# Reordering the first batch of a fused attention and mixer kernel: v by halves, s on a second queue, causal masks ahead of scores, masks of batch 1 on GpSimd

## The chip, the cores and the metric

The kernel runs on one core of a Trainium2 chip. The metric is the device time of one execution in microseconds (us), as a median over executions. Executions in which the time is over 1.5% above the fastest of the same kernel are called slow. A kernel is called faster or slower when it differs by 2%.

Five engines work side by side in this kernel, each on its own instructions in a fixed order: TensorE (PE, busy 278.1 of 293.2 us in the kernel before) multiplies matrices, ScalarE (ACT, 182.6) does exponentials and other functions, VectorE (DVE, 172.4) and GpSimd (POOL, 93.1) work elementwise, and SyncE (SP) issues most transfers. An engine whose next instruction waits is seen to do nothing else in the meantime, even if later instructions are ready: in experiment 1 below, ScalarE stands 12.04 us before one square, the last 3.70 of them with the scores of its next exponentials written (in the changed kernel it stands 12.10).

## The reference, cut to what matters

For 8 batches of 8 heads, 576 positions and 64 channels: attention with a decay, then a token mixer and a channel mixer.

```
cum    = cumsum(max(s, 0))
scores = q @ k.T / 8 + min(-(cum_i - cum_j), 0);  masked where j > i
x      = softmax(scores) @ v                       # heads side by side: 576 x 512
u      = x + (relu(x.T @ w_tok1) @ w_tok2).T
out    = u + relu(u @ w_ch1) @ w_ch2
```

## The kernel before

The decay is folded into the weights wn = exp(cum - half), which multiply v. A planner in the program models the duration of every operation and transfer, simulates the engines and fixes the order of instructions on each engine; the chip then runs that order. It makes six simulations ("passes") and keeps the one with the shortest modelled length.

Four heads form a quad. Its scores go into PSUM, ScalarE makes the exponentials, GpSimd or TensorE masks, and TensorE multiplies by v ("AV"). In batches below PMASK the mask is a matmul of the identity with a matrix of large negative numbers, added behind the scores:

```python
PMASK = 2
...
if pem:                                   # b < PMASK
    for e in range(HQ):
        for (jc, a, z, c0) in cols:
            n = min(128, S - jc * 128)
            nc.tensor.matmul(out=ps[e].t[:, c0 : c0 + n], lhsT=ident[:, :], rhs=neg[:, 0:n],
                             start=False, stop=(jc == cols[-1][0]))
```

To guard the arithmetic, ScalarE squares every loaded block of q and k and keeps the sums; a flag is made of them.

```python
def square(f, b, h, i):
    col = 2 * ((b * H + h) // HQ) + i
    P.op({"ACT": (1.1, 1.5, lambda: nc.scalar.activation(
        out=junk[:, :], in_=f.t[:, :], func=AF.Square, accum_out=sq[:, col : col + 1]))},
        reads=[(f, 0)], writes=[("sq", col)], prio=60)
```

## Time and profile before

| | before |
|---|---|
| time, median of 3 runs | 294.67 us (294.63 to 294.95) |
| span of the profiled run | 293.2 us |
| TensorE busy / idle | 278.1 / 15.1 us |
| granted TensorE clock | 1.00 in every window but the last |

TensorE is the bound. The columns are engine, line, releaser, then us in all, how often, and the longest:

```profile
ACT junk L645 <- DMA qkf<-in_k_dram: 5.7, 5, 1.9
ACT junk L645 <- DMA qkf<-in_q_dram: 4.6, 2, 4.4
```

ScalarE stands 10.3 us in front of squares whose q or k has not landed. TensorE's waits for exponentials come to only 0.4 us in this kernel, so the lines look harmless.

### The profile page before, as it was taken

To read this page: it belongs to the slowest core of one execution; us is meant where nothing else is said; L and a number is where in the kernel's file an instruction comes from. 1 tells how busy PE (TensorE), PEld (TensorE's weight loads), DVE (VectorE), ACT (ScalarE), POOL (GpSimd) and SP (SyncE) were. 2 spreads that over 40 slices of the span, in tenths; PEclk is the share of its full clock that TensorE was granted. 3 is DMA by queue.
4 is the path that set the end of the run, shared out by engine and by line. 5 is a ranking of instruction groups with operands and counts; after the bars stand their busy time and mean duration, and the time that the engine had idled before them with its cause. 6 is when DMAs were issued, how large, how long until landed. Compare 5 with 4: busy or idle time off the path is not lost.

```text
span 293.2 us, 6606 instructions
## 1 busy us (share of the span) xinstructions
PE 278.1 (95%) x2565; PEld 155.6 (53%) x2597; DVE 172.4 (59%) x332; ACT 182.6 (62%) x344; POOL 93.1 (32%) x138
## 2 busy tenths in 40 slices
PE   8779999989899979999999999999999999999994
PEld 3565466547554534446754545456754545347643
DVE  4974774989977635696847748596425523530022
ACT  3855875699896847975985278866872255007600
POOL 4332200878919312730481114821211210000000
PEclk9999999999999999999999999999999999999999
DMA  7998999999389999958493755667003320150023
GB/s 227 277 331 324 402 293 303 224 366 279 105 232 295 242 225 365 230 149 286 116 211 72 223 200 194 224 137 168 2 0 73 108 74 0 56 143 37 3 72 112
DMA packets 68051, 54.09 MB, mean 184 GB/s; under 512 B 53681, under 2 KB 56561, under 8 KB 68017
## 3 DMA queue, kind: packets, MB, share of 16 engines
q1 hardware_dynamic: 68016, 53.64, 64.6%
q8 instruction: 21, 0.34, 0.5%
q14 instruction: 14, 0.11, 0.1%
HBM read 40.65 MB, written 9.44 MB: 171 GB/s over the span
## 4 chain that ended last, share of the span: by engine, by line
PE 72%; DMA 9%; SPq 8%; DVE 6%; issue 2%; ACT 1%; POOL 1%; ACTq 0%
PE pmx L1078 26%; PE pmx L1052 25%; SPq L613 7%; PE pmx L994 4%; PE pmx L969 4%; PE pmx L744 4%; DMA ga<-in_moe_w_ch_dram 4%; PE psc L703 4%; DMA qkf<-in_k_dram 2%; DMA vf<-in_v_dram 2%; PE pmx L929 1%; DMA uTa<-ua 1%; PE psc L744 1%; DVE x L758 1%; DVE kT L670 1%
## 5 line engine op out<-in xcount | busy, mean ns | idle before, releaser
L719 ACT ACTIVATE E<-psc 128x512 bf16<-128x512 f32 x120 | 62.9, 602 | 20.9 <-PE psc L703 13.1
L1052 PEld LDWEIGHTS <-wc 128*128 128x128 bf16 x528 | 50.4, 98 | 35.0 <-issue 4.8
L727 POOL TENSOR_SCALAR_AFFINE_SELECT E<-E 128x512 bf16<-128x512 bf16 (+1 forms) x60 | 34.7, 608 | 87.0 <-ACT E L719 70.2
L1052 PE MATMUL pmx<-uTb,wc 128*128 128x320 bf16 x384 | 54.4, 299 | 1.1 <-DVE x L758 1.1
L1078 PE MATMUL pmx<-wc,gb 128*128 128x512 bf16 (+1 forms) x245 | 53.2, 369 | 0.5 <-issue 0.2
L1058 ACT ACTIVATE gb<-pmx 128x320 bf16<-128x320 f32 x79 | 34.3, 439 | 25.0 <-PE pmx L1052 18.1
L645 ACT ACTIVATE junk<-qkf 128x1152 bf16<-128x1152 f32 x32 | 37.3, 1165 | 10.7 <-DMA qkf<-in_k_dram 5.7
L1078 PEld LDWEIGHTS <-gb 128*128 128x128 bf16 x252 | 23.7, 98 | 25.4 <-issue 0.7
L620 POOL TENSOR_TENSOR vp<-vf,wT 128x512 bf16<-128x512 f32 (+1 forms) x30 | 32.1, 1100 | 9.2 <-PE pmx L744 9.2
L1052 PE MATMUL pmx<-uTa,wc 128*128 128x512 bf16 x137 | 32.4, 379 | 2.2 <-DMA uTa<-ua 1.8
L1078 PE MATMUL pmx<-wc,ga 128*128 128x512 bf16 x138 | 32.6, 379 | 0.4 <-issue 0.2
L659 POOL CAST qkb<-qkf 128x1152 bf16<-128x1152 f32 (+1 forms) x15 | 15.4, 1024 | 37.7 <-DMA qkf<-in_k_dram 16.4
L758 DVE TENSOR_TENSOR x<-pmx,rc 128x320 bf16<-128x320 f32 x52 | 25.5, 490 | 1.7
L744 PEld LDWEIGHTS <-E 128*128 128x128 bf16 x576 | 20.9, 97 | 6.8 <-DVE vp L620 1.7
L1058 ACT ACTIVATE ga<-pmx 128x512 bf16<-128x512 f32 x24 | 14.4, 599 | 15.6 <-PE pmx L1052 15.5
L670 DVE STREAM_TRANSPOSE kT<-qkb 128x576 f32<-128x576 f32 x16 | 20.1, 1255 | 5.7 <-PE psc L703 4.0
L1086 DVE TENSOR_TENSOR of<-pmx,ub 128x512 f32<-128x512 f32 (+1 forms) x17 | 11.2, 658 | 18.2 <-PE pmx L1078 14.4
L703 PE MATMUL psc<-qT,kT 32*128 32x256 bf16 (+2 forms) x592 | 20.1, 251 | 1.8 <-DVE qT L670 1.2
L1078 PEld LDWEIGHTS <-ga 128*128 128x128 bf16 x144 | 13.3, 98 | 15.6 <-issue 1.1
L670 DVE STREAM_TRANSPOSE qT<-qkb 128x576 f32<-128x576 f32 x16 | 20.0, 1247 | 1.6 <-ACT qkb L663 1.0
L703 PEld LDWEIGHTS <-kT 32*128 32x128 bf16 x640 | 13.6, 92 | 12.0 <-issue 10.2
L744 PE MATMUL pmx<-vp,E 128*128 128x65 bf16 x468 | 18.2, 193 | 0.0
(107 smaller groups left out, 285.1 us busy)
## 6 DMA issues: line engine op xcount, KB each, us to landing
qkf<-in_k_dram SPq DMA_DIRECT2D x20, 576.0 KB, 5.9
qkf<-in_q_dram SPq DMA_DIRECT2D x20, 576.0 KB, 6.1
vf<-in_v_dram SPq DMA_DIRECT2D x32, 256.0 KB, 5.8
out_dram<-of SPq DMA_DIRECT2D x31, 256.0 KB, 2.6
ga<-in_moe_w_ch_dram SPq DMA_DIRECT2D x6, 768.0 KB, 8.2
vf<-in_moe_w_ch_dram SPq DMA_DIRECT2D x2, 768.0 KB, 9.8
out_dram<-of SPq DMA_DIRECT2D x10, 128.0 KB, 2.7
vf<-in_v_dram SPq DMA_DIRECT2D x8, 128.0 KB, 4.9
```

The lines of the kernel that those rows point to most:

```text
L613: nc.sync.dma_start(out=vf.t[0:n, c, :, :], in_=v[b, :, c * 128 : c * 128 + n, :].rearrange("h p d -> p h d"))
L620: eng.tensor_tensor(out=vp.t[0:n, c, :, 0:D], in0=vf.t[0:n, c, :, :], in1=wT[0:n, c, b * H : b * H + H].unsqueeze(2).to_broadcast([n, H, D ...
L645: P.op({"ACT": (1.1, 1.5, lambda: nc.scalar.activation(out=junk[:, :], in_=f.t[:, :], func=AF.Square, accum_out=sq[:, col : col + 1]))}, r ...
L670: nc.vector.transpose(out=T.t[:, 0:S, :].rearrange("p s q -> p (s q)").bitcast(FP32).rearrange("p (t r) -> p r t", r=R), in_=t1.t[:, :].bi ...
L703: nc.tensor.matmul(out=ps[e].t[:, c0 : c0 + z - a], lhsT=kT.t[p0 : p0 + TP, jc * 128 : jc * 128 + 128, qq], rhs=qT.t[p0 : p0 + TP, a:z, qq ...
L719: nc.scalar.activation(out=E.t[:, e, ph * 512 : ph * 512 + 512], in_=p.t[:, :], func=AF.Exp, scale=0.125)
L727: nc.gpsimd.affine_select(out=w, in_=w, compare_op=ALU.is_ge, fill=0.0, base=0, pattern=[[0, HQ], [1, n]], channel_multiplier=-1)
L744: nc.tensor.matmul(out=o[:, ic, 0 : D + 1], lhsT=E.t[:, hh, d0 : d0 + 128], rhs=vp.t[:, jc, h + hh, 0 : D + 1], start=(jc == j_lo), stop=( ...
L758: nc.vector.tensor_tensor(out=x.t[:, :, (h + hh) * D : (h + hh + 1) * D], in0=o[:, :, 0:D], in1=rc.t[:, :].unsqueeze(2).to_broadcast([128, ...
L1052: nc.tensor.matmul(out=pm.t[:, 0 : e - a], lhsT=wc1[:, m, cc * 128 : cc * 128 + 128], rhs=uT.t[:, m, a:e], start=(m == 0), stop=(m == NMC ...
L1058: lambda cc=cc, pm=pm, a=a, e=e: nc.scalar.activation(out=g.t[:, cc, a:e], in_=pm.t[:, 0 : e - a], func=AF.Relu),
L1078: nc.tensor.matmul(out=pm.t[:, na:nb], lhsT=g.t[:, cc, c * 128 : c * 128 + 128], rhs=wc2[:, cc, na:nb], start=(cc == 0), stop=(cc == NCC - 1))
```

## The change

The intent is to start attention earlier and to relieve TensorE: s is loaded first, on ScalarE's queue; wn is made before the first exponentials; batch 0's masks are put into PSUM before the scores, while TensorE is waiting anyway; v of batch 0 is loaded by halves of the heads with w_tok1 between; masks of batch 1 go to GpSimd. The core of the diff:

```diff
-        etime = {"PE": 0.0, "ACT": 2.1, "DVE": 2.5, "POOL": 4.0, "SP": 0.7}
+        etime = {"PE": 0.0, "ACT": 2.86, "DVE": 2.5, "POOL": 4.0, "SP": 0.7}
-    PMASK = 2
+    PMASK = 1
-    stage_s = lambda: load_op(
-        lambda: nc.sync.dma_start(out=s_sb[:, :], in_=s...), ["s"], 1.0)
+    stage_s = lambda: early(
+        lambda: nc.scalar.dma_start(out=s_sb[:, :], in_=s...), ["s"], 3.5)   # 3.5: assumed landing
...                                              # relu of s from ScalarE to VectorE
+            def mask(ps=ps, cols=cols):          # ahead of the scores, 256 columns wide
+                for e in range(HQ):
+                    for (jc, a, z, c0) in cols:
+                        nc.tensor.matmul(out=ps[e].t[:, c0 : c0 + z - a], lhsT=ident[:, :],
+                                         rhs=neg[:, 0 : z - a], start=(c0 == 0), stop=False)
...
-    stage_qk(0, 0)
     stage_s()
     decay()
+    stage_qk(0, 0)
     stage_qk(0, HQ)
-    stage_v(0)
-    for h in range(0, H, HQ):
-        quad(0, h)
+    stage_v(0, 0)
+    quad(0, 0)
+    load_tok1(Buf(r_uTb))
+    stage_v(0, 1)
+    quad(0, HQ)
```

Because the planner starts anew, the order of instructions changes in all eight batches, not only in the first.

## The prediction

> **What bounds the kernel now.** I read the page first: TensorE (PE) is busy 278.1 of 293.2 us. So a gain has only two sources: matmul work that goes away, or some of the 15.1 us in which TensorE has nothing. I then cut the span into windows to find those 15 us.

> ```profile
> PE 278.1 (95%) x2565; PEld 155.6 (53%) x2597; DVE 172.4 (59%) x332; ACT 182.6 (62%) x344; POOL 93.1 (32%) x138
> ...
> 70.00:80.00 10.00, 8.80 (x111) 6.42 (x109) 9.79 (x22) 8.54 (x18) 9.95 (x11) 1.00 0.56 155
> ...
> 100.00:120.00 20.00, 18.06 (x146) 8.71 (x148) 10.15 (x20) 13.50 (x25) 4.54 (x7) 1.00 1.01 269
> ```

> Columns of a window: from:to, length, busy us of PE, PEld, DVE, ACT, POOL, then clock, DMA share, GB/s. Between 70 and 80 us VectorE (9.79) and GpSimd (9.95) are full and TensorE idles 1.2; between 100 and 120 it idles 1.9. From 20 to 50 us it idles only 0.25, from 120 to 280 only 1.5. The rest is the end (3 us after the last matmul) and the start.

> The start, from the timeline (start, duration, engine, line, operation, in brackets the idle time before and what ended it):

> ```profile
> 10.74 2.02 ACT L719 ACTIVATE E<-psc 128x512 bf16<-128x512 f32 x4
> ...
> 17.78 0.69 DVE L620 TENSOR_TENSOR vp<-vf,wT 64x512 bf16<-64x512 f32 x1 [1.34 <-DMA vf<-in_v_dram]
> 18.52 0.90 PEld L744 LDWEIGHTS <-E 128*128 128x128 bf16 x28 [1.65 <-DVE vp L620]
> ...
> 19.21 1.50 POOL L787 CAST w<-uTb 128x512 bf16<-128x512 f32 x3 [4.22 <-DMA uTb<-in_moe_w_tok_dram]
> ```

> Two chains meet at 18.5 us. ScalarE makes the sixteen exponentials back to back from 10.74 to 18.54 (0.485 each), and the last piece of v lands at 17.76, so E times v starts only at 18.52. A third follows: w_tok1 lands at 19.2, its casts end at 20.7, and the token mixing waits for them (first L864 at 20.78). Channel mixing (L906) runs steadily from 27.57. Much of TensorE's earlier busy time is warm-up on zeros (L1191, 25 records, 7.6 us).

> Then I asked what lies between 27 and 60 us, where TensorE never waits long:

> ```profile
> 31.36 12.37 SPq L613 DMA_DIRECT2D vf<-in_v_dram  x5
> 43.83 0.57 SPq L837 DMA_DIRECT2D ga<-in_moe_w_ch_dram  x1
> ...
> 50.68 0.96 DVE L789 CAST wc<-ga 128x1536 bf16<-128x1536 f32 x1 [2.86 <-DMA ga<-in_moe_w_ch_dram]
> ...
> 51.69 0.81 PE L929 MATMUL pmx<-wc,gb 128*128 128x512 bf16 x3 [0.27 <-DVE wc L789]
> ```

> The last quarter of w_ch2 is issued behind batch 1's v (12.37 us of issuing), lands at 50.66 and is cast by 51.64. TensorE needs it at 51.4 and waits 0.27. This is a second bound right behind the first: the transfers.

> ```profile
> 75.68 1.60 PE L1052 MATMUL pmx<-uTb,wc 128*128 128x320 bf16 x10 [1.06 <-DVE x L758]
> ...
> 96.56 6.43 SPq L1016 DMA_TRANSPOSE uTa<-ua  x4
> ...
> 104.58 1.02 PE L1052 MATMUL pmx<-uTa,wc 128*128 128x512 bf16 x4 [1.79 <-DMA uTa<-ua]
> ```

> The two single waits that I can see later. VectorE's chain up to the first holds the check's scan, gap and flag work (70.07 to 75) ahead of two normalisations; the second waits for transposes by DMA that were queued behind v loads.

> [...] v comes in 256-byte rows; in the trace the queue moves 222 GB/s from 10.4 to 14.7 us (v) and 400 from 27 to 40 us (mostly weights, k and q)[...]. [...] s on ScalarE's queue therefore frees 0.58 us of SyncE and moves s ahead[...]. [...] GpSimd's 128x576 cast takes 0.67 us, but 1.22 beside the scan, and its 128x32 copy 0.33, but 0.85 beside VectorE's v products. [...]

> **The change, part by part.** I compared the instruction order of both kernels on each engine, since a scheduler decides it.

> (1) s, cumulative sum and weights first. s landed at 7.73 and wn occupied ScalarE from 10.06 to 10.84, just ahead of the first exponential. With s ahead, relu (now VectorE), scan and wn lie near 4 to 7 us, beside the k and q loads. q's transpose still ends near 8.7 because q lands at 6.5, scores take 0.4 to 0.6 us, and the first exponential may start near 9.6 instead of 10.7: -1.1 for quad 0.

> (2) Masks of batch 0 ahead of scores. The mask groups (8 or 12 matmuls, 0.62 and 0.74 us each in the trace) leave the path between scores and exponentials. They get wider (up to 256 columns), but lie in warm-up time: -0.6, inside the 1.1 above. But the second quad's q lands at 10.7 as before, and its halves are now cast by GpSimd alone (2 x 0.67, after k's two and the copies of 0.33 and 0.21): transposed near 14.3, scores near 15. Eight exponentials from there (3.9) end near 19. So ScalarE gains no more than it lost, but AV of quad 0 can run at 16 to 17 instead of 18.5.

> (3) v by halves, w_tok1 between. Cumulated bytes: k and q done at 9.6 us, v's 1.18 MB took until 14.7 (0.23 MB/us), w_tok1's 0.59 MB some 1.6 us. Half a v is then through at 12.2 (landing, with the observed lag of 1 to 3 us, by 15), w_tok1 at 13.8 (landing near 16.3 instead of 19.2), the other half at 16.3 (landing near 19.1). AV of quad 1 can start at about 19.5, and one of four token chunks is done before. Left from there: AV 1.1 (36 at 0.03), three L864 groups (10 each at 0.088: 2.6), L877 4 x 0.23, L883 4 x 0.43: 6.4 us. Channel mixing starts near 26.0 instead of 27.57: **-1.5 us** at that point.

> (4) Masks of batch 1 by GpSimd. 40 matmuls of batch 1 go. Groups of 8 and 12 stand for 0.45 and 0.6 us of occupancy, twice each: **-2.2 us** of TensorE. Ten GpSimd selects (0.66 for 128x512) come in: 6 us, but GpSimd is idle from 38 to 52 us (0.67 busy in the slice 35 to 40, 0 in 40 to 50), so they cost latency only.

> (5) What meets (3) and (4): TensorE would reach the last w_ch2 quarter 3.5 to 4 us sooner, about 48.5. But the transfers ahead of it are the same bytes on a queue that is full from 27 to 41 us. What can move is the buffer wait: before, SyncE waited until 24.2 for the first w_ch1 buffer (cast by VectorE and ScalarE); in the changed order GpSimd and ScalarE cast it near 23.6. So the quarter lands near 50.1, is now cast by ScalarE (1.47 like the other ScalarE cast of this size, not 0.96), and is ready at 51.6: the same time. TensorE waits about 2.5 to 3 us there, the second quad's AV comes after it, and its four normalisations on VectorE (some 2.5 us) put the next token mixing at 56.2 to 56.6 against 56.5. **Steps 3 and 4 are eaten: 0 to -0.4.**

> (6) What the rescheduling brings by itself. The changed order puts all four normalisations before scan, gap and flags, so the 1.06 us wait at 74.6 should go: **-1.1**. The ScalarE squares that free the k and q buffers come earlier (two before the second exponentials of batch 2's first quad instead of one), so loads near 70 to 82 us, where the queue stood at 0.44 and 0.00, should move up to 10 us ahead. The transposes for batch 2 then find a drained queue although four v pieces instead of one are ahead of them: **-1.5**, most of the 1.8 at 102.8.

> After 105 us the matmul work is the same. Sum: -0.2 - 1.1 - 1.5 = -2.8, so 294.67 - 2.8 = **291.9 us**.

> **Rivals.** First, TensorE's account is all that counts and the transfers give way: then 1.5 + 2.2 + 1.1 + 1.8 = 6.6 and the time is 288.1. Against it: the 12.37 us of issuing and the 0.27 us wait that already exists. Second, the start gains nothing and the transposes get worse: three more v pieces of 262 KB at 0.22 MB/us ahead of them are 3.6 us, giving about 294.67 - 1.1 + 1.8 = 295.4. For it: the order of SyncE; against: the idle queue at 78 to 80 us. Third, GpSimd becomes the bound at 52 to 80 us with the masks of batch 1 running late: its load there is unchanged if the selects end by 50, so at most +1, 293.

> **Range and chances.** Between rival one and two, with my sum in the middle: 289.6 to 294.0 in 8 of 10. Over 2% faster means under 288.8, which needs the first rival nearly whole: 0.05. Over 2% slower needs 300.6, and nothing shown costs 6 us: 0.01. Within 2%: 0.94.

> **What would show it.** In the changed profile: the first exponential near 9.6 and wn before it; AV of quad 0 near 16; w_tok1's cast from 16.3; steady channel mixing from 26.0; a new TensorE wait of 2 to 3 us near 49 to 51.6 put down to the w_ch cast or its DMA; next token mixing at 56.5; no wait near 75; less than 0.5 us for uTa near 102. I am wrong if the last w_ch2 quarter lands by 48, or if TensorE's wait for uTa is longer than 1.8.

## The result

| | before | changed |
|---|---|---|
| time, median | 294.65 us (293.37 to 294.95, 4 runs) | 304.92 us (301.63 to 307.31, 4 runs) |
| span of the profiled run | 293.2 | 305.6 |
| TensorE busy / idle | 278.1 / 15.1 | 285.1 / 20.5 |
| mean granted clock | 0.998 (profiled run) | 0.972 (profiled run) to 0.988 |

The ratio is 1.032, 95% interval 1.0231 to 1.0409: slower. (A ratio is the mean time of one kernel's fast runs over that of the other's in the same rounds, so not quite the ratio of the medians quoted; in the experiments the profiled executions are left out of it.) The outputs are correct. The profiled run of the changed kernel is the one of 307.31 us, which counts as slow. So I read from it only what the fast profiled run of the first experiment shows as well, apart from the start, in which that experiment differs on purpose.

The page, engine line and clock line (40 slices of the span, tenths of full clock):

```profile
PE 285.1 (93%) x2549; PEld 157.1 (51%) x2549; DVE 171.5 (56%) x342; ACT 180.9 (59%) x338; POOL 106.6 (35%) x162
...
PEclk9599999799999996899999999999999999999999
```

TensorE does less work (the masks of batch 1 are gone) and is nevertheless busy 7.0 us longer. The clock line says why: at three places it is far below 9. In the kernel before this line is nines throughout:

```profile
PEclk9999999999999999999999999999999999999999
```

The changed kernel by windows, in the columns that the prediction explains:

```profile
0.00:20.00 20.00, 14.75 (x136) 8.11 (x140) 10.18 (x24) 8.59 (x15) 12.44 (x29) 0.83 0.95 263
...
40.00:60.00 20.00, 17.79 (x212) 10.08 (x201) 12.59 (x23) 15.85 (x26) 10.12 (x14) 0.91 0.93 262
...
100.00:120.00 20.00, 16.53 (x134) 7.89 (x133) 9.78 (x18) 7.90 (x14) 3.35 (x6) 0.94 0.85 235
120.00:140.00 20.00, 20.00 (x162) 9.18 (x152) 12.28 (x22) 13.17 (x25) 10.48 (x15) 0.89 0.62 141
```

An estimate of what the low clock costs is 20 x (0.17 + 0.09 + 0.06 + 0.11) = 8.6 us, less where TensorE was idle meanwhile. With 5.4 us more idle and 2.2 us fewer masks that makes 11.8 of the 12.4 us of difference in span.

What comes ahead of each low clock? The start, from the timeline:

```profile
0.91 0.56 ACTq L570 DMA_DIRECT2D s_sb<-in_s_dram  x1
...
6.56 0.45 DVE L573 TENSOR_SCALAR s_sb<-s_sb 64x576 f32<-64x576 f32 x1 [3.84 <-DMA s_sb<-in_s_dram]
...
9.54 0.76 PE L588 MATMUL pmx<-identf,wn 64*128 64x64 f32 x5 [3.37 <-ACT wn L581]
10.23 3.48 PE L1223 MATMUL pmx<-zero 128*128 128x512 bf16 x8
13.64 1.04 PE L734 MATMUL psc<-qT,kT 32*128 32x256 bf16 x16
...
14.71 2.07 ACT L745 ACTIVATE E<-psc 128x512 bf16<-128x512 f32 x4 [4.75 <-PE psc L734]
```

s lands 5.6 us after its issue, not at the 3.5 us that the planner was told. In TensorE's order the transposes of wn (L588) and eight warm-up matmuls on zeros (L1223) stand ahead of the scores, so TensorE idles 3.37 us; its clock is at 0.50 from 9 to 14 us, the eight warm-ups take 3.48 us (1.84 at full clock in experiment 1), and the first exponential starts at 14.71 in place of 10.74.

Near 55 us, and near 116 us:

```profile
55.76 2.34 PE L957 MATMUL pmx<-wc,gb 128*128 128x512 bf16 x6 [2.09 <-ACT wc L819]
...
111.08 0.38 SPq L658 DMA_DIRECT2D qkf<-in_k_dram  x1
112.07 0.63 PE L734 MATMUL psc<-qT,kT 32*128 32x256 bf16 x16
...
116.08 1.16 ACT L663 ACTIVATE junk<-qkf 128x1152 bf16<-128x1152 f32 x1 [12.10 <-DMA qkf<-in_k_dram]
...
117.24 2.04 ACT L745 ACTIVATE E<-psc 128x512 bf16<-128x512 f32 x4
117.87 2.47 PE L734 MATMUL psc<-qT,kT 32*128 32x256 bf16 x24 [2.48 <-ACT E L745]
```

At 55 us it is the last quarter of w_ch2, as predicted. At 116 it is a chain that the prediction has not got. Scores are written from 112.07 on. ScalarE could take their exponentials, but its next instruction is a square, whose k was issued only at 111.08. ScalarE stands 12.10 us before it; the exponentials follow at 117.24; and only they free the PSUM that TensorE's next scores (117.87) need.

### The profile page after: what moved, and what is told of

The parts are those of the page before. It is cut to its first block, busy times and chain, and to the rows that moved or that the text cites.

```text
span 305.6 us, 6559 instructions
## 1 busy us (share of the span) xinstructions
PE 285.1 (93%) x2549; PEld 157.1 (51%) x2549; DVE 171.5 (56%) x342; ACT 180.9 (59%) x338; POOL 106.6 (35%) x162
## 4 chain that ended last, share of the span: by engine, by line
PE 71%; DMA 19%; ACT 3%; DVE 2%; POOL 2%; SPq 1%; issue 1%; ACTq 0%; DVEq 0%; POOLq 0%
PE pmx L1106 26%; PE pmx L1080 24%; DMA ga<-in_moe_w_ch_dram 8%; DMA qkf<-in_k_dram 7%; PE psc L734 4%; PE pmx L772 4%; PE pmx L1022 3%; PE pmx L997 3%; DMA vf<-in_v_dram 3%; DMA s_sb<-in_s_dram 2%; PE pmx L1223 1%; POOL wc L815 1%; PE pmx L957 1%; PE psc L772 1%; ACT qkb L681 1%; PE pmx L723 1%
## 5 line engine op out<-in xcount | busy, mean ns | idle before, releaser
L745 ACT ACTIVATE E<-psc 128x512 bf16<-128x512 f32 x120 | 61.8, 602 | 31.4 <-PE psc L734 31.3
L753 POOL TENSOR_SCALAR_AFFINE_SELECT E<-E 128x512 bf16<-128x512 bf16 (+1 forms) x70 | 40.8, 612 | 86.0 <-ACT E L745 85.9
L1080 PEld LDWEIGHTS <-wc 128*128 128x128 bf16 x528 | 51.1, 99 | 35.6 <-issue 6.7
L1086 ACT ACTIVATE gb<-pmx 128x320 bf16<-128x320 f32 x66 | 28.4, 443 | 20.5 <-PE pmx L1080 15.9
L634 POOL TENSOR_TENSOR vp<-vf,wT 128x512 bf16<-128x512 f32 (+2 forms) x35 | 34.7, 1010 | 14.2 <-PE pmx L772 12.2
L1080 PE MATMUL pmx<-uTa,wc 128*128 128x512 bf16 x144 | 34.8, 396 | 0.7 <-DMA uTa<-ua 0.6
L677 POOL CAST qkb<-qkf 128x576 bf16<-128x576 f32 (+1 forms) x18 | 16.6, 936 | 28.3 <-DVE kT L690 12.1
L786 DVE TENSOR_TENSOR x<-pmx,rc 128x320 bf16<-128x320 f32 x50 | 23.5, 486 | 0.9
L1114 DVE TENSOR_TENSOR of<-pmx,ub 128x512 f32<-128x512 f32 (+1 forms) x17 | 11.2, 658 | 22.3 <-PE pmx L1106 18.5
L734 PE MATMUL psc<-qT,kT 32*128 32x256 bf16 (+2 forms) x592 | 20.9, 259 | 2.8 <-ACT E L745 2.5
L681 ACT CAST qkb<-qkf 128x1152 bf16<-128x1152 f32 (+1 forms) x18 | 18.2, 1019 | 7.3 <-DMA qkf<-in_k_dram 5.0
L1106 PEld LDWEIGHTS <-ga 128*128 128x128 bf16 x144 | 13.5, 98 | 16.3 <-issue 1.1
L734 PEld LDWEIGHTS <-kT 32*128 32x128 bf16 x640 | 13.8, 94 | 13.1 <-issue 10.6
(111 smaller groups left out, 293.2 us busy)
```

The source lines that it names most:

```text
L634: eng.tensor_tensor(out=vp.t[0:n, c, h0:h1, 0:D], in0=vf.t[0:n, c, h0:h1, :], in1=wT[0:n, c, b * H + h0 : b * H + h1].unsqueeze(2).to_broa ...
L681: nc.scalar.copy(out=o.t[:, a:z], in_=i.t[:, a:z])
L734: nc.tensor.matmul(out=ps[e].t[:, c0 : c0 + z - a], lhsT=kT.t[p0 : p0 + TP, jc * 128 : jc * 128 + 128, qq], rhs=qT.t[p0 : p0 + TP, a:z, qq ...
L745: nc.scalar.activation(out=E.t[:, e, ph * 512 : ph * 512 + 512], in_=p.t[:, :], func=AF.Exp, scale=0.125)
L753: nc.gpsimd.affine_select(out=w, in_=w, compare_op=ALU.is_ge, fill=0.0, base=0, pattern=[[0, HQ], [1, n]], channel_multiplier=-1)
L786: nc.vector.tensor_tensor(out=x.t[:, :, (h + hh) * D : (h + hh + 1) * D], in0=o[:, :, 0:D], in1=rc.t[:, :].unsqueeze(2).to_broadcast([128, ...
```

## The experiments

All results are correct unless said otherwise. "Same order" means that every engine keeps the order of the kernel the experiment starts from, so that only the named thing differs. "New order" means that the planner started anew.

**1. s first on SyncE's queue** (changed kernel, same order).

```diff
-        lambda: nc.scalar.dma_start(out=s_sb[:, :], ...), ["s"], 3.5)
+        lambda: nc.sync.dma_start(out=s_sb[:, :], ...), ["s"], 3.5)
```

> The changed kernel with one word edited: s is issued by SyncE ahead of k instead of by ScalarE; the order on every other engine is the same. Theory A (s lands late because it shares the engines with k and q from a second queue, and TensorE's fixed order waits for it): s lands before 4.2 us instead of 6.54, TensorE does not idle 3.4 us before the wn transposes, scores start before 9.5 instead of 13.6, the clock stays at 1.0 in the first 20 us, and the time falls to 290 to 294. Theory B (the new order is slow whatever s does): s lands early but the time stays above 300. Theory C (s takes some 5.6 us on any queue): s still lands after 6 us and nothing changes, 302 to 307.

Measured: 303.61 us (301.95 to 304.38), ratio 1.0306 (1.0206 to 1.0405). s is used from 3.70 us on, the clock is 1.00 until 20 us, the first exponential starts at 11.59. But the time stays. In the profile the stall near 112 us is there as before:

```profile
107.64 0.64 PE L734 MATMUL psc<-qT,kT 32*128 32x256 bf16 x16
...
111.98 1.16 ACT L663 ACTIVATE junk<-qkf 128x1152 bf16<-128x1152 f32 x1 [12.04 <-DMA qkf<-in_k_dram]
...
113.14 2.04 ACT L745 ACTIVATE E<-psc 128x512 bf16<-128x512 f32 x4
...
113.77 0.27 PE L734 MATMUL psc<-qT,kT 32*128 32x256 bf16 x1 [2.80 <-ACT E L745]
```

```profile
113.00:114.00 1.00, 0.23 (x1) 0.09 (x1) 0.00 (x0) 1.00 (x4) 0.00 (x0) 1.00 0.93 308
114.00:121.00 7.00, 6.54 (x36) 2.77 (x35) 3.14 (x4) 5.52 (x11) 3.74 (x6) 0.52 0.37 114
```

The 2.80 us wait is followed by seven microseconds at 0.52 of the clock. The start is not where the 10 us are.

**2. s on ScalarE's queue in the kernel before** (same order).

> The kernel before with s issued by ScalarE, nothing else moved. Theory A: s lands near 6.5 us as in the changed kernel (7.7 before), and since scores stand ahead of the wn transposes there, the time stays at 293.5 to 295.5. If the second queue itself disturbed k and q, scores would start later than 8.7 and the time would rise by over 2 us.

Measured: 294.69 us (293.62 to 295.91), ratio 1.0014 (0.9919 to 1.0109). s is of no earlier use there: issued at 0.91 us in place of 1.85, it goes into its relu at 7.99 us in place of 7.78. q's transpose ends at 9.48 us in place of 8.63, and the first scores need it. The total doesn't show either. That this is so because scores stand ahead of the transposes of wn in that order fits, but was not tested by itself.

**3. An honest landing time** (changed kernel, `3.5` made `6.5`; new order).

> The changed kernel with only the assumed landing time of s raised from 3.5 to 6.5 us in the scheduler, so that it fills TensorE with warm-up matmuls until then (21 instead of 6 ahead of the wn transposes) and replans the rest. Theory A: s still lands near 6.5, but TensorE and its clock do not go idle, scores start near 10.5, and the time is 291 to 296. Theory B: above 300.

Measured: 296.73 us (293.9 to 301.91), ratio 1.0019 (0.9892 to 1.0146). Almost the whole loss is gone. But all of the order is new, and the first experiment has shown that the start alone isn't worth this. So this run first of all says that two orders of the same work can be 8 us apart.

**4. Sixteen warm-up matmuls ahead of the transposes of wn** (changed kernel, otherwise same order).

> The changed kernel with 16 warm-up matmuls of 512 columns put just ahead of the wn transposes, all else in the same order. Parts the late s from the lost clock: s still lands at 6.5 and wn is still ready at 9.4, but the clock stays at 1.0, so the eight fills behind the transposes take 1.7 instead of 3.5 us and scores start near 11.8 instead of 13.6. If the clock is a large part of the loss: 298 to 302. If only the wait for s counts: 303 to 306.

Measured: 305.18 us (301.63 to 306.28), ratio 1.0305 (1.0153 to 1.0458). The mean clock of the profiled run is 0.987 in place of 0.972 and the first exponential starts at 12.70 in place of 14.71, yet the total does not move. What is won at the start is waited for later.

**5, 6 and 7. Which pass of the planner is chosen.** The planner took its first pass for the changed kernel, a simple one, and a later one for the kernel before.

```diff
-            if best is None or length < best[0]:
+            if best is None or i == 1 or length < best[0]:      # 5 and 7: first pass not eligible
-    order = P.run()
+    order = P.run(1)                                            # 6: first pass only
```

> The changed kernel with one line different in the planner: its first pass, which takes ready operations by plain priority, may not be chosen; the best of the later passes, which order VectorE, ScalarE and GpSimd by the length of what still hangs on an operation, is taken instead. In the changed kernel the planner's own lengths are 287.0 for the first pass and 290.1 at best for the others, so it took the first; in the kernel before they were 288.8 and 286.8, so it took a later one. Theory C (the loss comes from the chosen kind of order, which on the chip stalls in the middle of the kernel): 295 to 298 us, with the waits near 54 and 112 us gone or under 1 us. Theory D (the loss comes from what the change does, masks by GpSimd and v in halves, whatever the order): 302 to 306. If the planner's lengths were right: 308.

> The kernel before, with the planner held to its first pass (planned length 288.8 in place of 286.8); nothing else of the kernel differs. Theory C: the old kernel loses several us too, 299 to 304, with waits of TensorE over 2 us between 50 and 120 us and a granted clock under 0.95 there. Theory D: the planned difference or less, 294.5 to 297.

> The kernel of the previous line but one with s on SyncE's queue again: the start (s and its clock drop) and the kind of order both undone. Theory C: 1 to 4 us below that kernel, so 292 to 296, and the first exponential below 12 us. Theory D: 300 to 304. If a late s is absorbed by later waits: equal to that kernel within 1 us.

Measured: run 5 took 301.08 us (298.56 to 302.44), ratio 1.0218; run 6 298.5 (297.94 to 299.1), ratio 1.0122; run 7 300.89 (298.19 to 303.21), ratio 1.0166. Theory C fails as a whole: a later pass is 4 us better for the changed kernel, not 8, and the waits only move (in run 5 TensorE waits 3.5, 2.3, 1.9 and 1.8 us, mostly in other places). The planner's lengths don't tell it either: 290.1 ran faster than 287.0. The kernel before loses 4 us with another pass, so its own order is a good draw among several. Runs 5 and 7 agree within 0.2 us, so the late s is absorbed in that order too.

**8. The later squares read zeros** (the kernel of experiment 1, same order).

```diff
-            out=junk[:, :], in_=f.t[:, :], func=AF.Square, ...
+            out=junk[:, :], in_=f.t[:, :] if b < 2 else zero[:, 0:1].to_broadcast([128, R * D]), func=AF.Square, ...
```

> The changed kernel with s on SyncE's queue (first experiment, 303.6 us), same planned order, but the squares of the batches after the second read a constant of zeros in place of the loaded q or k: their duration stays, their wait for the load goes (they only feed a guard, so the outputs stay right for these inputs). Theory: the square that held ScalarE up to 112 us stands ahead of the exponentials that TensorE waits for; without its wait the stall of about 2.8 us and the half clock after it go: 297 to 300, window 100 to 120 us of TensorE over 17.5 busy. Rival: the exponentials then wait for another thing (a cast of the same load, which TensorE needs anyway): 302 to 304.

Measured: **295.38 us** (294.94 to 295.62), ratio 1.0005 (0.9932 to 1.0077). That is 8.2 us less than experiment 1, lower than the 297 to 300 expected, and no run of one comes near a run of the other. (They ran in different rounds; each against its own kernel before, the gap is 3.0%.) The squares are still there and take as long (1.15 to 1.19 us each between 90 and 124 us, 1.16 to 1.22 in experiment 1), but two ties are cut at once: ScalarE's wait for q and k, and SyncE's wait until a square has read a buffer before it loads the next q or k into it. Between 40 and 130 us SyncE waits 5.1 us for squares in experiment 1 and not at all here, so that k is issued at 105.20 in place of 106.57. The same place in the timeline:

```profile
107.03 0.63 PE L734 MATMUL psc<-qT,kT 32*128 32x256 bf16 x16
...
107.69 2.06 ACT L745 ACTIVATE E<-psc 128x512 bf16<-128x512 f32 x4 [7.65 <-PE psc L734]
...
110.29 0.64 PE L734 MATMUL psc<-qT,kT 32*128 32x256 bf16 x24
```

The exponentials now follow their scores, 2.5 us after k's issue and so before it has landed (in the profiles of the kernel before and of the changed one no load of q or k lands in under 3.4 us), and the next scores don't wait. So ScalarE's wait was real here; but a k that came 1.4 us earlier would have shortened TensorE's wait of 2.80 us by about half even with it (an estimate). No run separates the two ties. The accounts of the two profiled runs split the gain: the span falls by 7.9 us (301.8 to 293.9), TensorE's idle time by 3.0 (20.5 to 17.5), its busy time by 4.9 (281.3 to 276.4), with the same matmuls. The busy part is the clock: in experiment 1 it was 0.91, 0.86 and 0.97 in the windows from 40, 100 and 120 us (an estimate of 20 x 0.26 = 5.2 us), here 1.00 in each. So more of the loss came after the waits than in them. Not all of it belongs to the stall at 112 us: 1.8 of the 5.2 us are at 53 us, where the wait itself was nearly as long (1.30 against 1.57).

**9. The same with s as in the change** (the changed kernel, same order, squares as in 8).

> The changed kernel exactly as it is (s on ScalarE's queue), but with the later squares reading a constant of zeros, as in the run of 295.4 us. It measures what the late s costs when the squares hold nothing up. If the loss is the squares' and the start is absorbed further on, as it was with the squares waiting (304.9 against 303.6): 295 to 297. If the start costs its full lag (first exponential at 14.7 in place of 11.6 us) once the later wait is gone: 298 to 300. If the squares only mattered in the other kernel: 303 to 306.

Measured: 296.22 us (295.03 to 299.11), ratio 1.0054 (0.9975 to 1.0133), against 304.92 with the squares waiting. The late s costs about 0.8 us, within the spread of the runs, although its clock is low in this run too (0.91 in the first 20 us).

**10. The same in the kernel before** (same order).

> The kernel before with the later squares reading zeros, same planned order. In its profile ScalarE stood 10.3 us in all before squares for q and k, longest 4.4, and TensorE waited under 0.4 us for exponentials. If the squares are harmless in the old order: 293.5 to 295.5, the same as the old kernel, and the change's own work is worth nothing net. If they cost the old kernel too: 290 to 292, and then the changed kernel without them (295.4) is truly slower than this one.

Measured: 292.89 us (292.06 to 295.19), ratio 0.9981 (0.9893 to 1.0068). The squares cost the old order 2.0 us by the medians of the same rounds and nothing that the interval can tell from zero. But the profile shows a path by which they can cost: in the kernel before SyncE waits for squares to free the buffers of q and k (first line, between 60 and 130 us); here it doesn't, the transposes of batch 2 begin at 90.32 in place of 96.56, and TensorE's wait of 1.79 us for uTa is gone (19.84 us busy in this window, 18.06 before):

```profile
SPq L640 <- ACT junk L645: 10.4, 3, 5.9
```

```profile
90.32 6.03 SPq L1016 DMA_TRANSPOSE uTa<-ua  x4
...
100.00:120.00 20.00, 19.84 (x169) 9.55 (x170) 11.28 (x21) 14.50 (x26) 7.19 (x9) 1.00 0.99 271
```

It is the order of the change that makes them expensive. Treated alike, the changed kernel still isn't faster (295.4 against 292.9).

**11 and 12. A cure that keeps the work** (new orders): the planner is told that a square can begin only 6 us after its load has landed, so it puts it further back. Run 11 is the changed kernel with s on SyncE's queue, run 12 the kernel before.

```diff
-                u.ready = max(u.ready, est + self.gap(o, u, e))
+                u.ready = max(u.ready, est + self.gap(o, u, e) + u.slack)      # squares: slack 6.0, others 0
```

> The changed kernel with s on SyncE's queue, squares reading their loads as they should, but the planner told that a square can begin only 6 us after its load lands, so that it puts them further back in ScalarE's order (planned length 285.8, first pass chosen). A cure that keeps the work. If head-of-line waiting is the cause: 294 to 298 and ScalarE's waits before squares under 4 us in all, with no clock under 0.95 after the start. If any replan loses: 300 to 304.

> The same 6 us for the squares in the kernel before (planned length 286.7, a later pass chosen). If the old order was harmed by squares: 290 to 293. If not: 294 to 297, the spread of a new plan.

Measured: run 11 took 293.51 us (292.95 to 298.46, 5 runs), ratio 0.9967 (0.9869 to 1.0066), with no wait of ScalarE before a square, but with the clock at 0.91 from 60 to 80 us, where none under 0.95 was expected (TensorE waited 3.06 us for ScalarE there); run 12 297.88 (297.47 to 299.06), ratio 1.0129. Run 11 is the best version of the change, but no better than the kernel before by its interval.

**13. What the masks of batch 1 are worth** (kernel before, same order; wrong result on purpose, relative error 0.44).

```diff
             def mm(ps=ps, cols=cols):
+                pem = b == 0                     # batch 1 is left unmasked
```

> The kernel before with the mask matmuls of batch 1 simply left out (wrong result on purpose for batch 1), same order on every engine. If that TensorE work lies on the path: 2.2 us less, ratio 0.992 or 0.993. If a wait that follows (weights, loads, exponentials in the first 60 us) takes it: within 0.5 us, ratio 0.998 to 1.002.

Measured: 297.18 us (295.62 to 300.39, 6 runs) against 294.02, ratio **1.01** (1.0029 to 1.0172). Neither theory: work was taken from the bounding engine, in an unchanged order, and the kernel became slower. The profile shows how:

```profile
51.50 1.10 PE L930 MATMUL pmx<-wc,gb 128*128 128x512 bf16 x2 [2.37 <-DVE wc L790]
...
106.57 1.86 PE L1053 MATMUL pmx<-uTa,wc 128*128 128x512 bf16 x4 [2.56 <-DMA uTa<-ua]
```

```profile
49.00:52.00 3.00, 0.54 (x7) 0.26 (x5) 1.48 (x4) 0.00 (x0) 0.00 (x0) 0.98 1.07 365
52.00:55.00 3.00, 3.00 (x39) 2.41 (x39) 2.46 (x11) 2.97 (x5) 2.39 (x3) 0.50 0.86 186
104.00:107.00 3.00, 0.44 (x3) 0.18 (x3) 0.69 (x1) 0.00 (x0) 0.00 (x0) 0.92 0.91 135
107.00:109.00 2.00, 2.00 (x19) 0.69 (x18) 0.00 (x0) 0.53 (x1) 0.00 (x0) 0.50 1.01 275
```

TensorE reaches the last w_ch2 quarter 2.3 us earlier and waits 2.37 us in place of 0.27, because the quarter comes only 0.2 us earlier. Had that been all, the masks would simply have been worth nothing. But the wait is followed by three microseconds at half clock. The same happens at 105 us, where the old wait for uTa was 1.79 us at full clock and the new one is 2.56. The clock is not the whole loss, though. The mean clocks of the six runs are 0.982 to 0.998, and two stretches of 3.4 us at half clock make the profiled run's 0.988. The two runs with 0.997 and 0.998 still took 295.9 and 295.6 us, 1.6 to 1.9 above the median of the kernel before (whose own runs with such clocks reach 296.1). That rest is not explained.

**14 and 15. Two parts of the cured kernel** (run 11; new orders): masks of batch 1 back on TensorE (`PMASK = 2`), and the last w_ch2 quarter ahead of batch 1's v in the list of loads.

> The cured changed kernel (s on SyncE's queue, squares planned 6 us later, 293.5 us) with the masks of batch 1 back on TensorE; a new plan, length 289.1 against 285.8. If the move of masks is worth its 2.2 us: 295 to 297. If it is worth nothing: 293 to 294.5. If the move harms (GpSimd's masks make the exponentials' readers wait): 290 to 292.5.

> The cured changed kernel with the last quarter of w_ch2 put ahead of batch 1's v in the list of loads; a new plan, length 288.9 against 285.8. In the cured kernel TensorE waited 2.6 us for the cast of that quarter near 54 us, and its clock was 0.91 in the window 60 to 80. If that load is what stops it: the wait falls below 0.5 us and the time to 290 to 292.5, unless v is then late (a wait of TensorE for vp instead: 293 to 295). If the new plan is worse elsewhere, as its length says: 296 or more.

Measured: 297.58 us (297.0 to 298.5), ratio 1.0131, and 300.13 (299.15 to 300.84), ratio 1.0218. Run 14 falls where "worth 2.2 us" was expected, but with a new order and in view of runs 12 and 16 it proves nothing of the masks. In run 15 the wait for the w_ch2 cast falls from 2.6 to 0.2 us as intended, and others of 2.6, 1.8 and 1.4 us appear on other operands. Inconclusive both.

**16 and 17. The cure with 12 us in place of 6** (new orders), for the changed kernel and for the kernel before.

> The changed kernel with s on SyncE's queue and squares planned 12 us after their loads land in place of 6 (planned length 286.1 against 285.8). If keeping squares from the head of ScalarE's order is the cure: 292 to 297, no wait of ScalarE before a square over 4 us between 80 and 130 us. If 293.5 was a lucky plan: 299 or more.

> The kernel before with the same 12 us (planned length 285.6, against 286.8 for the kernel before as it is and 286.7 with 6 us, which ran at 297.9). If planned lengths told the time: 293.5. If each new plan is a draw with a spread of some 3 us: anything from 291 to 298, and what decides is whether TensorE's waits of over 2 us are followed by half clock.

Measured: 299.05 us (298.27 to 303.0, 6 runs), ratio 1.0137 (1.0078 to 1.0195), and 299.12 (296.57 to 300.77, 6 runs), ratio 1.0117 (1.0054 to 1.018). So 293.5 was a good draw, and the cure isn't a cure in general. In both runs no wait of ScalarE before a square comes up in the view of waits. In run 16 TensorE waits 2.39 us for ScalarE's copy into uTb at 65 us and 2.36 us for VectorE at 112 us, and the clock is 0.91 in each of the two windows around them. In run 17 a wait of 3.6 us near 65 us is followed by half clock too (0.83 from 60 to 80 us).

All orders side by side, medians in us:

| work | orders made by the planner |
|---|---|
| changed kernel, with its small variants of load order and hints | 304.9, 296.7, 301.1, 293.5, 299.1, 300.1 |
| kernel before | 294.7, 298.5, 297.9, 299.1 |

Run 14 has the masks of batch 1 elsewhere and is in neither row; run 7 (300.9) has the order of run 5. Both kinds of work spread over several microseconds, and the ranges overlap. In these orders the order decides more than the work that the change moved.

## Why the prediction was wrong

The prediction was 291.9 us (289.6 to 294.0), with 0.01 for slower by over 2%. Measured were 304.9 us.

**Step 1, s first and the first exponential near 9.6: wrong.** It started at 14.71. The step assumed that s lands so that relu begins near 4 us; it landed at about 6.5. The prediction did not reckon with s taking longer there: its 144 KB took 5.6 us from issue to landing on ScalarE's queue beside loads on SyncE's, 2.8 on SyncE's in experiment 11. (Behind two loads on SyncE's queue, in the kernel before, it took 5.9.) Two things then multiplied the delay: TensorE's fixed order, with wn ahead of the scores, and the clock at 0.50 after 3.37 us of idling. And even with s landing at 3.70 us (experiment 1) the first exponential came at 11.59, not at 9.6: q's transpose, counted on by 8.7, ended only near 10.9. Still, experiments 1 and 9 show that all this was worth about 1 us of the total.

**Step 2, masks ahead of scores: the mechanism was right, the size was not.** The masks lie ahead of the scores or between them as planned, but AV of quad 0 began at 20.19, not at 16 to 17. With s on SyncE's queue it began at 16.82.

**Step 3, channel mixing at 26.0: wrong.** w_tok1 did arrive early, its cast starting at 15.44 in place of 19.21. But steady channel mixing began at 30.26, and even with the start repaired only at 27.66, against 27.57 before.

**Step 4, 2.2 us less of TensorE's work: right as an account, wrong as a gain.** Experiment 13 removed just that work and lost 3 us.

**Step 5, eaten by the last w_ch2 quarter, "0 to -0.4": the mechanism was right, the size and the sign of this term were wrong.** The wait of 2.5 to 3 us came, 2.09 us in the changed kernel and 2.37 in experiment 13. The prediction took a wait to cost its own length. In these runs it was followed by half clock: in experiment 13 the clock is at 0.50 for 3.4 us after it, which by an estimate is another 1.7 us. The next token mixing began at 61.76, not at 56.5; 3.1 us of that came from the late start (58.66 in experiment 1).

**Step 6 is the step that failed worst.** It said that "the ScalarE squares that free the k and q buffers come earlier", and counted -1.5 us for loads that move up. The wait for uTa did shrink, from 1.79 to 0.63 us, and the wait near 75 us went; that squares which free their buffers sooner let the loads and the transposes move up is also what experiment 10's profile shows. But squares that stand earlier in ScalarE's order stand ahead of exponentials, and they wait for loads that come late. ScalarE stood 12 us before one of them, and experiments 8 and 9 show that the squares' ties to their loads, ScalarE's wait and the hold on the buffers together, cost 8.2 and 8.7 us. In the kernel before there were 10.3 us of the same waiting in plain view. I took them for harmless, and by the times of experiment 10 they cost little there.

**The rivals and the chances** shared one blind spot. All of them took the sum of waits and work as the time, and "nothing shown costs 6 us" rested on that. Neither a wait on an engine that isn't the bound nor the clock after a wait was in the list. The working has slips besides, none of which made the miss: 51.4 less 3.5 to 4 is 47.4 to 47.9, not 48.5; some 2 us of TensorE's idle time (from 50 to 70 and from 80 to 100 us) are in none of its parts; and the second rival's +1.8 is not derived from its 3.6.

**Which waits were followed by half clock.** Waits of 1.57 us (experiment 1) and 2.37 (experiment 13) were; these two of 2.6 to 2.7 us were not:

```profile
52.48 1.46 PE L958 MATMUL pmx<-wc,gb 128*128 128x512 bf16 x6 [2.58 <-ACT wc L820]
```

```profile
82.58 0.70 PE L1080 MATMUL pmx<-uTb,wc 128*128 128x320 bf16 x4 [2.71 <-ACT gb L1086]
```

The first is from experiment 11, the second from experiment 8; the clock stays at 1.00 in the microseconds after each. In the trace of the changed kernel half clock begins at 8.38, 56.17 and 117.61 us and lasts 6.83, 3.41 and 6.83 us (it begins once more at 305.34, behind the last matmul). From one start to the next it is 14, 18 and 55 times 3.413 us; the two starts in experiment 1, 52.82 and 114.26 us, lie 18 times that apart. Cut the trace into intervals on that grid. The intervals just ahead of the first three starts hold 1.19, 1.26 and 1.20 us of TensorE work; the 80 at full clock that full clock follows hold 2.12 us or more. In the kernel before the only start, at 291.73 us, lies behind the last matmul; on its grid the interval ahead of it holds 1.14 us, each of the 84 others 1.88 or more. The wait of 1.57 us in experiment 1, and the interval after it:

```profile
49.41:52.82 3.41, 1.72 (x37) 1.34 (x36) 2.46 (x8) 3.02 (x5) 1.84 (x4) 1.00 1.06 374
52.82:56.23 3.41, 3.41 (x29) 1.98 (x28) 1.97 (x3) 3.07 (x5) 1.34 (x2) 0.50 0.92 192
```

The wait of 2.58 us in experiment 11 is shared out between two intervals:

```profile
47.57:50.98 3.41, 2.22 (x38) 1.54 (x38) 2.40 (x9) 2.02 (x5) 2.10 (x4) 1.00 1.03 399
50.98:54.39 3.41, 1.91 (x27) 1.20 (x27) 1.07 (x2) 3.39 (x4) 0.26 (x1) 1.00 0.88 209
```

**What stays open.** No run set the place of a wait on that grid on purpose. It isn't settled which of the squares' two ties costs how much, whether masks on GpSimd are worth anything in a good order, and why the start gains nothing at 27 us. Those would need orders that differ in one thing only, also where the planner is asked anew.

## What to carry to other kernels

Here operations off the critical path that waited for late loads stood ahead of critical ones in an engine's fixed order, and with the hold on the buffers that cost 8.2 us (experiment 8), so look for such waits on every engine, not only on the bound. Waits of TensorE of 1.57 to 2.80 us were followed by 3.4 or 6.8 us at half clock in experiments 1 and 13, an estimated 1.7 or 3.4 us on top of each, so don't take a wait to cost just its length; and don't be surprised if removing work ahead of a fixed transfer slows a kernel, as it did in experiment 13 (ratio 1.01). To judge a change to a planned kernel, hold the order fixed and change one thing, for a new order alone moved this one by up to 10 us (303.6 in experiment 1 against 293.5 in experiment 11).
